# Retention and cosine MLP on one core: the first k in two transfers, part of the first v on another queue, and a new plan

## The chip, the cores and the metric

The kernel runs on one core of a Trainium2 chip. The metric is the time of one execution on the device, in microseconds (us), lower is better. The kernel before took 209.12 us, the median of three runs (208.57 to 209.28). A profiled execution took 208.1 us, of which the profile's span covers 206.3. All times of single instructions below are from that profile.

## The reference

Two layers follow each other. The first is a recurrent retention over 768 time steps, for 4 batch elements and 8 heads of 64 channels; the second multiplies its output (3072 tokens of 512) by w_in (512 x 2048), applies h * cos(h), and multiplies by w_out (2048 x 512).

```python
for t in range(S):
    state = gamma * state + k[t] (outer) v[t]
    y[t] = scale * q[t] @ state
x = y as (tokens, heads * channels)
h = x @ w_in
out = (h * cos(h)) @ w_out
```

All inputs and the output are float32.

## The kernel before

**Tiles.** Time is cut into 6 chunks of 128 steps, and the batch into 2 pairs. A slot p is one chunk of one pair, so there are 12 slots; slots 0 and 1 are the first chunk of each pair. In a slot, the recurrence becomes matrix products: q and k are transposed on TensorE (`t_mm`, line 361) and copied back (`t_copy`), the scores of each head are multiplied (`a_mm`, line 399 for the first two slots, 389 later), masked with the decay (`a_mask`, or `a_save` and `a_late` through ScalarE and GpSimd), and multiplied with v (`y_first`, line 431, for the first two slots; `y_block` later). The state between chunks is kept in one PSUM bank (`s_mm`, line 578). The output of a slot is copied, transposed, into `xt` (`y_copy`).

**The MLP.** Two slots make a group of 512 tokens. A unit of work multiplies 512 tokens by 128 columns of w_in (`f_mm`, line 590), or, where only one slot is there yet, 256 tokens by two times 128 columns (`h_mm`, line 611). ScalarE takes the cosine (`f_cos`), VectorE the product (`f_mul`, `h_mul`), and `o_mm` (line 635) multiplies by w_out. `HALF0` says how many of the 16 column blocks of group 0 are done as half units.

**Loads.** q of slot 0 comes by SyncE's hardware queue in two halves, one for each batch element of the pair. Nearly everything else in the first 60 us is issued by GpSimd, through the software queue: `load(p, "K")` or `"Q"` casts to bf16 on the way (slots 0 and 1), `"q"`, `"k"`, `"v"` bring float32, which an engine converts (`conv_q`, `conv_k`, `conv_v`, and `raw_v`, a plain cast of v for slots 0 and 1). Names with a digit, such as `q0`, load one batch element; in the kernel before, only q is loaded so. GpSimd works through its instructions in order, so issues, conversions and masks stand in one line there.

**The plan.** The order of the first half (slots 0 to 6, group 0 and the start of group 1) is made while the kernel is built: `Plan.run` is a list scheduler with a cost for each operation, tokens for PSUM banks and buffers, a rank for each operation, and assumed times of landing (`ld`, `at`). The constants `SHIFT` and `ON` change ranks and choose engines; they were searched for. Where TensorE has nothing to do between 4.2 and 18 us of the plan's own time, it puts in `idle_mm` (line 664), a product of zeros into a free bank that keeps the array running. The instructions are then emitted in the plan's order, and the chip keeps only this order, not its times: every engine executes in order and waits on semaphores. From group 2 on the order is a fixed loop.

**What the change touches:** the loads of slot 0 (`load`, and the two calls ahead of the plan), the table of assumed landings `ld` and the list `LOADS`, the constants, and with them the order of the whole planned half.

Of the kernel before, what the change touches and what calls it, by code (L numbers as in the profile page):

```python
# [161 lines left out]
            op["fn"](op["eng"])  # L162


HOLD = ""
SHIFT = {"ml010": 25.5, "mulf0.2": -74.7, "f0.3": 0.3, "cosf0.2": -11.6, "cosf0.3": -2.2, "mulf0.3": -4.9, "f0.2": 2.8, "m011": -20.0, "mulh1.4": -20.5, "m000": 82.7, "cosf0.5": -41.6, "ck21": 45.1, "a31": -124.5, "m100": 2.2, "f0.5": 23.0, "a5": -2.5, "v0": -97.2, "ms110": 6.4, "ml110": -41.8, "cosf0.4": -0.9, "f0.4": -9.8, "mulf0.5": 16.9, "eq51": 13.1, "m110": 64.4, "t20": -21.1, "k5": -46.0, "mulf0.8": 31.6, "yc21": -50.4, "f0.6": 2.1, "f0.7": 55.3, "ek10": -92.1, "w0b": -22.2, "a21": -34.2, "h1.0": 81.4, "cosh2.2": 3.0, "m501": 38.5, "yc30": -23.3, "ml011": -27.8, "mulf0.15": 5.8, "sc5": 79.1, "m201": -81.3, "mulh2.2": -18.0, "oc1": -45.8, "mulf0.14": -66.8, "cq31": -32.2, "mulf0.9": -47.9, "mulf0.6": 5.7, "cosf0.7": -27.8, "a30": -8.1, "cosf0.6": -7.2, "h0.2": -12.1, "eq21": -4.6, "cq51": 3.2, "cq41": 38.6, "f0.14": 23.8, "ek20": -13.4, "yc50": 39.8, "cv51": 23.4, "ek51": 88.5, "mulh2.10": 23.3, "cq70": 8.6, "f0.10": -46.0, "mulf0.13": 1.5, "h1.6": 5.9, "ml100": 20.1, "f0.15": 60.8, "o2.1": -8.1, "h3.10": 31.9, "t51": 14.8, "h3.0": -7.1, "h3.14": 28.8, "cq00": -2.7, "m601": 4.7, "h1.4": 1.8, "eq11": 37.0, "cosf0.12": -60.7, "v6": -26.4, "m400": 17.7, "mulh3.12": 67.0, "w2": 49.4, "sw": -53.6, "cv10": -0.0, "rv00": 14.5, "mulh2.8": 4.5, "ek50": 72.2, "cosf0.11": 2.4, "m101": -34.4, "h2.2": 1.1, "q2": -22.9, "q5": -59.7, "cosh3.14": 19.9, "y3": 19.8, "t40": 30.7, "o2": -0.8, "mulh3.4": -0.3, "cq40": -13.2, "mulh0.2": -29.3, "y5": -35.7, "mulh3.14": -25.5, "h2.12": -50.9, "oc0": -94.2, "a10": 39.9, "ek11": -35.3, "h0.6": 6.9, "eq40": -6.2, "h2.6": 58.1, "rv10": -9.1, "dt71": -1.3, "cosh3.8": -31.0, "cosh0.2": 18.8, "cv70": -67.6, "o3.1": -13.8, "cq60": -11.1, "ck60": 71.1, "m511": 10.9, "sc4": -15.9, "o1.3": -16.8, "m510": 4.5, "k4": 12.5, "h0.4": -9.2, "cq71": 3.6, "mulh3.2": 58.9, "cosh1.2": -26.7, "mulh3.6": -1.4, "cv61": 13.7, "o2.2": -9.8, "q6": -7.4, "o0.2": -7.5, "mulh2.4": 44.5, "mulh2.6": 22.6, "mulh3.10": 16.6, "v5": -53.7, "cq61": 27.8, "o1.1": -27.2, "ck61": 0.2, "m200": -10.8, "cosf0.9": 6.3, "cosh0.4": 11.6, "q4": 78.9, "cosh3.6": -6.8, "h1.2": -87.9, "tq01": 1.8, "oc3": -74.8, "mulh0.0": -16.9, "eq01": 11.2, "t21": 6.2, "ck41": 29.7, "cosh3.4": 9.3, "oc2": 8.6, "m211": 23.9, "cq01": -56.9, "w0a": 17.8, "o1.0": -7.7, "yc01": 2.2, "k7": 54.8, "yc51": -0.7, "cosf0.13": -14.9, "cosh2.10": -36.4, "yc00": 7.1, "cosh1.4": -13.4, "ek00": -8.7, "m611": -13.9, "tk10": -101.4, "mulh0.4": -40.7, "mulf0.10": 15.2, "m600": -35.2, "a00": -17.4, "cosh2.0": -5.5, "m301": 18.6, "rv11": -50.0, "sc0": -52.0, "ek01": -31.6, "cv01": 13.3, "ek21": -3.2, "cosf0.10": 7.2, "v7": -2.1, "ek40": 18.1, "t31": 22.7, "mulh1.6": 0.2, "eq30": -9.4, "y4": 19.2, "tk11": 1.9, "ek31": -26.9, "w3b": 23.5, "cosh2.12": -0.2, "cosh0.6": 4.7, "cosh2.8": -4.4, "cosh3.2": 25.8, "cv60": 2.7, "cosh2.4": -14.4, "v4": -1.1, "mulh2.12": 36.6, "dt61": -8.8, "eq41": -12.5, "mulf0.11": 31.8, "ek41": -0.8, "eq50": 9.1, "a11": -23.9, "yc10": 9.3, "o0.3": 0.3, "dt60": -3.3, "o3.3": 50.5, "mulh2.14": -42.3, "m610": -12.1, "f0.11": -0.6, "s0": 3.1, "cv11": 38.9, "h3.8": -17.4, "yc40": 14.3, "m410": -8.4, "h2.8": -4.0, "m300": 15.8, "o0": -14.6, "cv31": -27.4, "rv01": 0.6, "cosf0.14": 2.4, "cosh2.6": 11.7, "cv50": -6.8, "m010": -1.2, "ms011": -12.0, "f0.13": -5.2, "l8": 5.1, "ck70": 3.2, "t41": 1.0, "o1.2": -2.3, "cv71": 0.5, "tq11": 31.2, "h2.4": -3.6, "mulh0.6": 8.8, "t50": 7.1, "ck31": 42.7, "yc20": -52.3, "m001": -4.7, "y01": 62.0, "y2": 15.3, "f0.12": 20.5, "ms111": 2.0, "mulh1.2": -13.9, "cosh3.10": -49.0, "ck51": -9.0, "h0.0": -0.1, "eq31": 1.4, "eq20": -5.1, "q7": 1.5, "cosh3.0": 6.2, "cosh3.12": 1.5, "cv40": 2.3, "y11": 3.6, "o1": -24.4, "cv00": -1.4, "sc2": -3.2, "m411": 18.0, "m210": -8.1, "v3": 0.0, "eq10": 1.1, "tk01": 22.8, "yc41": -25.6, "cq21": -1.8, "f0.9": -31.4}
ON = {"cv70": "P", "cv00": "D", "cv30": "D", "cv31": "D", "cv60": "D", "cv11": "D", "cv10": "P", "rv01": "D", "sc5": "D", "rv11": "A", "yc20": "D", "sc3": "D", "eq40": "DA", "eq50": "A", "rv00": "A", "yc00": "D", "yc31": "DA", "ek51": "D", "ek11": "DA", "sc4": "D", "ek20": "A", "cv61": "P", "eq01": "DA", "cv51": "D", "ek41": "D", "eq41": "A", "cv20": "P", "yc01": "DA", "eq20": "A", "eq30": "DA", "ek50": "D", "ek00": "D", "sc2": "DA", "yc50": "DA", "yc40": "A", "yc21": "A", "cq21": "D", "ek40": "DA", "cv01": "D", "cv71": "P", "cv21": "P", "ek21": "DA", "cv41": "P", "cq20": "D", "ek10": "DA", "yc30": "A", "ek01": "D"}
HALF0, SPARE, RF, RM, COLD = 8, 1, 50.0, 50.0, 5.2


@with_exitstack
def kernel(
# [9 lines left out]
    nc = tc.nc  # L182
    B, H, S, D = q.shape
# [9 lines left out]
    PRE = 5  # L193
# [70 lines left out]
    def kb(p):  # L264
        return by_b(kx if p == 1 else ks[p % NB], p)
# [6 lines left out]
    def load(eng, p, names):  # L272

        bp, c = divmod(ORDER[p], NC)
        for n in names.split():
            t, src = SRC[n[0].lower()]
            if len(n) == 1:
                t = (qb(p) if n == "Q" else kb(p)) if n in "QK" else t[p % PRE]  # L280
                eng.dma_start(  # L281
                    out=t.rearrange("p b h d -> p (b h) d"),
                    in_=src[ds(2 * bp, 2), :, ds(c * C, C), :].rearrange(
                        "b h t d -> t (b h) d"))
            elif n[1] == "s":
                fl = t[p % PRE].rearrange("p b h d -> p (b h) d")
                for x in range(2):
                    for lo, n4, th in ((0, 4, x), (4, 8, 1 - x), (12, 4, x)):
                        eng.dma_start(
                            out=fl[ts(x, 64), ds(lo, n4), :],  # L290
                            in_=src[ds(2 * bp, 2), :, ds(c * C + 64 * th, 64), :]
                            .rearrange("b h t d -> t (b h) d")[:, ds(lo, n4), :])
            else:
                b = int(n[1])
                eng.dma_start(
                    out=t[p % PRE][:, b],
                    in_=src[2 * bp + b, :, ds(c * C, C)].rearrange("h t d -> t h d"))

    def load_w_in(lo, n):
# [362 lines left out]
    def idle_mm(e, n=1):  # L662
# [10 lines left out]
                   allow_small_or_imprecise_dtypes=True)  # L673
    nc.gpsimd.iota(far[:, 8:24], pattern=[[1, 16]], base=0, channel_multiplier=0,
                   allow_small_or_imprecise_dtypes=True)
    load(nc.sync, 0, "q0 q1")
    load(nc.gpsimd, 0, "K")
    nc.vector.memset(zero, 0.0)
    nc.vector.memset(lnsc, math.log(scale))
    nc.vector.memset(halfpi, math.pi / 2.0)  # L680
# [2 lines left out]
        out=dist.rearrange("p (a b) -> p a b", a=8),  # L683
# [20 lines left out]
    PL = 6  # L704
    ASEP = 4
    MERGE = 4
    CQ, CD = "P", "DP"
    SPLIT = {(1, 1, 1), (0, 1, 1)}
    HM, HCQ, HCV = "q2", "", ""
    plan = Plan({"bank": 7, "cos": 3, "sem": 8, "out": 4, "port": 1, "ring": 7}, 6.5)  # L710
    add = plan.add
    SB2 = {"D": (0.33, 0.42), "A": (0.49, 0.585)}
    TT = {"D": (0.6, 0.69), "P": (1.03, 1.05)}
# [1 line left out]
    ld = {}  # L715
    prev = None
    at = lambda tm: dict(start=0.0, free=0.0, done=tm, lat=0.0)
    ld["q", 0, 0], ld["q", 0, 1], ld["k", 0, 0], ld["k", 0, 1] = map(at, (3.9, 5.0, 7.4, 7.4))
    LOADS = ["Q1", "K1", "v0", "v1", "w0a", "w0b", "w1", "w2", "q2", "k2", "w3a", "v2", "w3b", "o0", "q3", "k3", "v3", "o1", "q4", "o2", "k4", "v4", "q5", "k5", "o3", "v5", "q6", "k6", "v6", "q7", "k7", "v7"]
    LAG = {"w1": 0.15}  # L720
    pend = []
    for i, x in enumerate(LOADS):
        if x[0] in "qkvQK":
            p = int(x[1:])
            o = add("P", 1.2, lambda e, p=p, n=x[0]: load(nc.gpsimd, p, n),
                    [("issued", prev)] if prev else [], 50 + i if p < 7 else 45,
                    [("sem", 1), ("ring", 1)], [("sem", 1), ("ring", 1)], mb=524288e-6, rate=330e-3, name=x)
            ld[x[0].lower(), p, 0] = ld[x[0].lower(), p, 1] = o
            if p >= PRE:
                pend.append((o, x[0], p - PRE))  # L730
        elif x[0] == "w":
# [16 lines left out]
    for p in range(PL + 2):  # L748
# [92 lines left out]
        else:  # L841
# [4 lines left out]
                    name="y%d" % p)  # L846
# [151 lines left out]
```

## Time and profile before

| engine | busy us | share of the span |
|---|---|---|
| TensorE, matmuls (PE) | 201.4 | 98% |
| TensorE, weight loads (PEld) | 108.6 | 53% |
| VectorE (DVE) | 114.2 | 55% |
| ScalarE (ACT) | 115.2 | 56% |
| GpSimd (POOL) | 73.8 | 36% |

| landing at the start | issued by | first used at us |
|---|---|---|
| q of slot 0, first batch element | SyncE | 3.76 |
| q of slot 0, second | SyncE | 4.64 |
| k of slot 0 | GpSimd, from 1.41 for 1.38 us | 7.17 |
| q of slot 1 | GpSimd, 2.79 | 8.86 |
| k of slot 1 | GpSimd, 3.92 | 10.71 |
| v of slot 0 | GpSimd, from 5.06 | 12.23 |
| v of slot 1 | GpSimd, after it | 13.94 |

How to read it: an engine that is busy for 98% of the span sets the time, but busy is not the same as useful. The 34 products of zeros are in the 201.4 us as well: seven while the kernel starts, the others between 4.26 and 15.19 us. The second table gives the time of the first instruction that reads the data, which may be later than the landing. In tables of stretches of time ("windows") the columns are: the stretch, its length, the busy time of PE, PEld, DVE, ACT and POOL with the number of instructions, the granted clock of TensorE, the mean share of busy DMA engines (over 1 where transfers overlap), and GB/s written. A line of waits has the engine and line that waited, what ended the wait, the sum in us, the count and the longest.

### The profile page before, as it was taken

What the parts mean: (1) busy time and instruction counts of PE and PEld (TensorE: products, weight loads), DVE (VectorE), ACT (ScalarE), POOL (GpSimd) and SP (SyncE); (2) the same over time, 40 slices, a digit from 0 to 9 for tenths busy, and PEclk for the clock granted to TensorE, in tenths of its full rate; (3) what the DMA queues carried; (4) which work ended last, traced back from release to release, by engine and by line L of the source; (5) the groups of instructions that cost most, each with busy time, mean ns of one, the idle gap of its engine ahead of it and who ended that gap; (6) DMA issues with size and microseconds to landing.
All of it is one profiled execution on the core that took longest, in us unless ns stands there. A gap on an engine that the chain in (4) does not pass through costs nothing.

```text
span 206.3 us, 5229 instructions
## 1 busy us (share of the span) xinstructions
PE 201.4 (98%) x2178; PEld 108.6 (53%) x2178; DVE 114.2 (55%) x194; ACT 115.2 (56%) x193; POOL 73.8 (36%) x77
## 2 busy tenths in 40 slices
PE   7999999999999999999999999999999999999994
PEld 2558656868945545445445445454444444444442
DVE  5589897866996548338338438448442444444000
ACT  7567886859855357547546546554555553554120
POOL 8969979899973004305207005200000000000000
PEclk9999999999999999999999999999999999999999
DMA  7999999999998976876877675501101101110212
GB/s 121 186 262 210 314 241 312 255 342 276 344 312 150 231 158 175 201 193 171 192 177 144 151 193 142 153 0 56 53 1 51 51 3 51 51 51 0 104 53 102
DMA packets 58600, 32.15 MB, mean 156 GB/s; under 512 B 47696, under 2 KB 53072, under 8 KB 58576
## 3 DMA queue, kind: packets, MB, share of 16 engines
q0 software_dynamic: 14352, 15.47, 33.9%
q1 hardware_dynamic: 44080, 16.28, 31.1%
q8 instruction: 17, 0.28, 0.6%
q10 hardware_dynamic: 144, 0.07, 0.1%
q14 instruction: 7, 0.06, 0.1%
HBM read 27.26 MB, written 6.29 MB: 163 GB/s over the span
## 4 chain that ended last, share of the span: by engine, by line
PE 78%; DMA 10%; POOL 7%; DVE 2%; issue 1%; ACT 1%; POOLq 0%; DVEq 0%
PE bank L635 37%; PE bank L590 27%; DMA vf<-in_v_dram 10%; PE bank L611 4%; PE bank L389 2%; PE bank L480 2%; PE bank L655 2%; DVE gt L619 1%; PE st_ps L508 1%; POOL qf L281 1%; POOL kf L281 1%; PE bank L494 1%; PE bank L361 1%; POOL w_in_sb L300 1%; POOL ks L281 1%
## 5 line engine op out<-in xcount | busy, mean ns | idle before, releaser
L598 ACT ACTIVATE cosb<-bank,halfpi 128x512 bf16<-128x512 f32 x96 | 65.6, 690 | 53.2 <-PE bank L590 48.0
L635 PE MATMUL bank<-w_out_sb,gt 128*128 128x512 bf16 x368 | 90.9, 379 | 0.0
L602 DVE TENSOR_TENSOR gt<-bank,cosb 128x512 bf16<-128x512 f32 x72 | 49.1, 690 | 55.8 <-ACT cosb L598 55.7
L590 PE MATMUL bank<-xt,w_in_sb 128*128 128x512 bf16 x288 | 73.2, 379 | 0.0
L635 PEld LDWEIGHTS <-gt 128*128 128x128 bf16 x368 | 35.5, 98 | 42.3 <-issue 0.2
L590 PEld LDWEIGHTS <-w_in_sb 128*128 128x128 bf16 x288 | 27.6, 98 | 32.3
L324 POOL TENSOR_TENSOR qs<-qf,gq 128x512 bf16<-128x512 f32 x18 | 18.5, 1044 | 43.5 <-PE bank L480 22.6
L408 DVE TENSOR_TENSOR am<-bank,mask 128x512 bf16<-128x512 f32 x40 | 24.8, 682 | 4.2 <-PE bank L389 4.2
L313 ACT COPY ob<-bank 128x512 f32<-128x512 f32 (+1 forms) x24 | 14.0, 582 | 16.0 <-PE bank L635 13.9
L611 PE MATMUL bank<-xt,w_in_sb 128*128 128x256 bf16 x192 | 22.3, 273 | 0.0
L611 PEld LDWEIGHTS <-w_in_sb 128*128 128x128 bf16 x192 | 18.5, 98 | 3.1
L619 DVE TENSOR_TENSOR gt<-bank,cosb 128x512 bf16<-128x512 f32 x24 | 16.0, 686 | 4.7 <-ACT cosb L598 4.6
L313 ACT CAST xt<-bank 128x512 bf16<-128x512 f32 x21 | 11.4, 588 | 10.8 <-PE bank L480 10.1
L313 ACT CAST ks<-kf 128x512 bf16<-128x512 f32 x20 | 11.5, 625 | 2.7 <-DMA kf<-in_k_dram 2.7
L664 PE MATMUL bank<-zero 128*128 128x512 bf16 x34 | 10.5, 442 | 1.1 <-DVE halfpi L680 1.1
L480 PE MATMUL bank<-am,vs 64*64 64x128 bf16 (+1 forms) x320 | 10.3, 206 | 0.1
L336 POOL TENSOR_TENSOR vs<-vf,gk 128x512 bf16<-128x512 f32 x8 | 8.9, 1113 | 3.3 <-PE bank L480 1.5
L331 POOL TENSOR_TENSOR vs<-vf,gk 128x512 bf16<-128x512 f32 x8 | 8.2, 1042 | 5.2 <-DMA vf<-in_v_dram 3.8
L281 POOL DMA_DIRECT2D vf<-in_v_dram x8 | 9.4, 1182 | 1.0 <-DVE vs L336 0.8
L315 DVE CAST stb<-st_ps 128x512 bf16<-128x512 f32 x9 | 6.2, 687 | 3.8 <-PE st_ps L508 3.3
L389 PE MATMUL bank<-qkt 64*64 64x128 bf16 (+1 forms) x320 | 8.0, 206 | 0.3 <-ACT qkt L313 0.2
L313 ACT COPY qkt<-bank 128x512 bf16<-128x512 bf16 x13 | 7.1, 592 | 1.8 <-PE bank L361 1.2
(66 smaller groups left out, 132.7 us busy)
## 6 DMA issues: line engine op xcount, KB each, us to landing
out_dram<-ob SPq DMA_DIRECT2D x23, 256.0 KB, 2.4
vf<-in_v_dram POOLq DMA_DIRECT2D x8, 512.0 KB, 12.0
qf<-in_q_dram POOLq DMA_DIRECT2D x6, 512.0 KB, 12.5
kf<-in_k_dram POOLq DMA_DIRECT2D x6, 512.0 KB, 12.4
w_out_sb<-in_moe_w_out_dram POOLq DMA_DIRECT2D x4, 512.0 KB, 14.1
qf<-in_q_dram SPq DMA_DIRECT2D x4, 512.0 KB, 4.6
w_in_sb<-in_moe_w_in_dram POOLq DMA_DIRECT2D x4, 256.0 KB, 8.7
w_in_sb<-in_moe_w_in_dram POOLq DMA_DIRECT2D x2, 512.0 KB, 10.5
```

The source lines that it names most:

```text
L281: eng.dma_start(out=t.rearrange("p b h d -> p (b h) d"), in_=src[ds(2 * bp, 2), :, ds(c * C, C), :].rearrange("b h t d -> t (b h) d"))
L313: nc.scalar.copy(out=out, in_=in_)
L324: ENG[e].tensor_tensor(out=qb(p)[:, b], in0=qf[p % PRE][:, b], in1=bc(gq, ORDER[p] % NC), op=ALU.mult)
L389: return nc.tensor.matmul(ap[b][ts(x, 64), a, lo:], lhsT=kt(p % NB, b, h)[:, ts(x, 64)], rhs=qt(p % NB, b, h)[:, lo:], tile_position=(64 * ...
L408: nc.vector.tensor_tensor(out=am[p % 2][b][u], in0=bank.rearrange("p (a t) -> p a t", a=HP), in1=(dec[:, b] if p < 2 else mask[second(p, 0 ...
L480: m = nc.tensor.matmul(held["yp", p][b][ts(j, 64), a, lo:], lhsT=vs[p % NB][ts(r, 64), b, h, :], rhs=am[p % 2][b][h // 4][ts(r, 64), h % 4 ...
L590: nc.tensor.matmul(bank, lhsT=w_in_sb[:, i, ts(f, 128)], rhs=xt[g % 2][:, i, :], start=(i == 0), stop=(i == KIN - 1))
L598: nc.scalar.activation(out=cb, in_=bank, func=AF.Sin, bias=halfpi)
L602: nc.vector.tensor_tensor(out=gt[g % 2][:, f, :], in0=bank, in1=cb, op=ALU.mult)
L611: nc.tensor.matmul(bank[:, ts(e, 256)], lhsT=w_in_sb[:, i, ts(f + e, 128)], rhs=xt[g % 2][:, i, ts(hf, 256)], start=(i == 0 and e == 0), s ...
L619: nc.vector.tensor_tensor(out=gt[g % 2][:, f : f + 2, ts(hf, 256)], in0=bank.rearrange("p (f t) -> p f t", f=2), in1=cb.rearrange("p (f t) ...
L635: nc.tensor.matmul(bank, lhsT=gt[g % 2][:, f, ts(j, 128)], rhs=w_out_sb[:, f, :], start=(f == 0), stop=(f == KOUT - 1))
```

## The change

k of slot 0 is loaded by two software transfers, one for each batch element, so that the first half can be issued, and used, before the second. v of slot 0 is split as well: its first batch element goes to SyncE's hardware queue, behind q; its second stays with GpSimd, in the place of the whole. The assumed landings follow: k at 6.4 and 6.9 (7.4 for both before), v's first element at 9.0, the software stream from 5.9 on (6.5 before). The list of loads gets another order: the first half of w_in's first 512 columns comes ahead of v of slot 1, and later weights move forward. `HALF0` falls from 8 to 4. With these, the plan's ranks and engines were searched for anew (`SHIFT`, `ON`, left out here).

```diff
-HOLD = ""
...
-HALF0, SPARE, RF, RM, COLD = 8, 1, 50.0, 50.0, 5.2
+HOLD = "P"
...
+HALF0, SPARE, RF, RM, COLD = 4, 0, 40.0, 50.0, 5.2
...
-                    out=t[p % PRE][:, b],
+                    out=(kb(p) if n[0] == "K" else t[p % PRE])[:, b],
...
-    load(nc.sync, 0, "q0 q1")
-    load(nc.gpsimd, 0, "K")
+    load(nc.sync, 0, "q0 q1 v0")
+    load(nc.gpsimd, 0, "K0 K1")
...
-    CQ, CD = "P", "DP"
-    SPLIT = {(1, 1, 1), (0, 1, 1)}
+    CQ, CD = "P", "P"
+    SPLIT = {(1, 1, 0), (0, 1, 1)}
...
-    plan = Plan({"bank": 7, "cos": 3, "sem": 8, "out": 4, "port": 1, "ring": 7}, 6.5)
+    plan = Plan({"bank": 7, "cos": 3, "sem": 8, "out": 4, "port": 1, "ring": 7}, 5.9)
...
-    ld["q", 0, 0], ld["q", 0, 1], ld["k", 0, 0], ld["k", 0, 1] = map(at, (3.9, 5.0, 7.4, 7.4))
-    LOADS = ["Q1", "K1", "v0", "v1", "w0a", "w0b", "w1", "w2", "q2", "k2", "w3a", "v2", "w3b", "o0", "q3", "k3", "v3", "o1", "q4", "o2", "k4", "v4", "q5", "k5", "o3", "v5", "q6", "k6", "v6", "q7", "k7", "v7"]
+    ld["q", 0, 0], ld["q", 0, 1], ld["k", 0, 0], ld["k", 0, 1] = map(at, (3.9, 5.0, 6.4, 6.9))
+    ld["v", 0, 0] = at(9.0)
+    LOADS = ["Q1", "K1", "v0", "w0a", "v1", "w0b", "w1", "w2", "q2", "w3a", "k2", "w3b", "v2", "o0", "o1", "q3", "k3", "v3", "o2", "q4", "o3", "k4", "v4", "q5", "k5", "v5", "q6", "k6", "v6", "q7", "k7", "v7"]
...
-            o = add("P", 1.2, lambda e, p=p, n=x[0]: load(nc.gpsimd, p, n),
+            half = x == "v0"
+            o = add("P", 0.7 if half else 1.2,
+                    lambda e, p=p, n="v1" if half else x[0]: load(nc.gpsimd, p, n),
...
-            ld[x[0].lower(), p, 0] = ld[x[0].lower(), p, 1] = o
+            for b in range(half, 2):
+                ld[x[0].lower(), p, b] = o
```

In the new list, `"v0"` stands for the second batch element of v of slot 0 alone.

## The prediction

> **What bounds the kernel now.** I read the page's first two parts first, then the windows of the start, then the timeline of TensorE, and last the waits of TensorE.
>
> ```profile
> PE 201.4 (98%) x2178; PEld 108.6 (53%) x2178; DVE 114.2 (55%) x194; ACT 115.2 (56%) x193; POOL 73.8 (36%) x77
> ...
> DMA  7999999999998976876877675501101101110212
> ```
>
> TensorE is busy for 201.4 of 206.3 us. The rest is 1.06 us ahead of its first instruction, 2.6 us of final write-out after its last, and about 1 us of gaps. So it is the bound, and the only ways to be faster are fewer useless matmuls and fewer gaps. Useless ones exist: line 664 multiplies zeros into a free bank, to keep the array running while nothing is there to compute.
>
> ```profile
> 13.00 0.64 PE L431 MATMUL bank<-am,gt 128*64 128x128 bf16 x16
> 13.57 1.69 PE L664 MATMUL bank<-zero 128*128 128x512 bf16 x7
> 15.19 0.64 PE L431 MATMUL bank<-am,gt 128*64 128x128 bf16 x16
> 15.76 1.92 PE L611 MATMUL bank<-xt,w_in_sb 128*128 128x256 bf16 x16
> 17.61 0.44 PE L578 MATMUL st_ps<-vs,ks 128*64 128x64 bf16 x16
> ```
>
> This is TensorE's timeline (start, length). L431 is the output of slot 0, then of slot 1; L611 is the first real w_in work. From 15.19 on there is no filler. Between 4.26 and 15.19 there are 27 fillers (groups of 2, 7, 2, 4, 3, 2 and 7). So the start is limited by landings, and the rest by TensorE's own work.
>
> ```profile
> 2.50:4.00 1.50, 1.50 (x5) 0.30 (x2) 0.68 (x9) 1.50 (x6) 1.50 (x3) 1.00 1.27 283
> 4.00:5.00 1.00, 0.97 (x6) 0.56 (x6) 0.56 (x2) 1.00 (x5) 1.00 (x1) 1.00 1.34 109
> 5.00:9.00 4.00, 3.96 (x42) 1.98 (x41) 1.82 (x5) 2.26 (x6) 4.00 (x6) 1.00 2.39 153
> 9.00:10.00 1.00, 1.00 (x12) 0.62 (x10) 1.00 (x3) 0.96 (x2) 1.00 (x2) 1.00 1.97 252
> 10.00:12.50 2.50, 2.14 (x30) 1.15 (x29) 1.52 (x4) 0.86 (x2) 1.64 (x2) 1.00 1.07 341
> ```
>
> The last column is GB/s written. k of slot 0, q and k of slot 1 are cast to bf16 on the way, so 153 written is 306 read: from 5 us on the DMA engines run at one rate, about 300 GB/s of source data. From 4 to 5 us, where k of slot 0 is the only long transfer, they do 109 (at most 218 read). That hole, and the wait of k for its descriptors, is what the change can win.
>
> ```profile
> PE bank L664 <- DVE halfpi L680: 1.1, 1, 1.1
> PE bank L361 <- DMA kx<-in_k_dram: 0.4, 1, 0.4
> PE bank L389 <- ACT qkt L313: 0.2, 1, 0.2
> ```
>
> TensorE's waits: after the start only 0.6 us in all. The present order is kept almost exactly by the chip.
>
> **What the Trainium skill says.** "DMA: Bandwidth & Descriptors", section "Specifications", gives about 1 us to the first byte on the software path and 0.6 us on the hardware path. The trace agrees in kind: k's issue ends at 2.79 us, and the written rate shows bf16 only from about 4.0. The same page, "Queues, rings and completion order", says that each DMA engine takes turns between the queues that it has work for, packet by packet. The trace is mixed: the small copies of gk and mask, issued by SyncE from 5.21 us, took 6.0 to 6.4 us to land, all that time beside the software stream. "TensorE: Matmul & The Clock Gate", section "What's actually happening", gives 215.7 ns from start to start of warm matmuls of 512 columns; four of L590 take 0.86 us in the chain here, 216 ns each, so a filler costs 0.216.
>
> **The change part by part.**
> *k of slot 0 in two software transfers.* The whole issue took 1.38 us on GpSimd, later ones of this kind 1.17; no row shows a half: between 0.59 (half of 1.17) and 0.8 (a w_in issue), I take 0.7. The first half is then issued by some 2.2 us instead of 2.79, and its data starts 0.6 earlier, inside the hole. k landed at 7.17 (first matmul on it); the first half should now land 0.8 to 1.1 us earlier, the second 0 to 0.5. GpSimd pays two halves for one whole, nothing.
> *v of batch element 0 on SyncE, behind q.* A third issue of 0.54 us (1.08 for two) behind which only the gk and mask copies wait, needed much later: free. It takes 256 KB out of the software stream. When does it land? At best one q half after q's second, 4.64 + 0.88 = 5.5; at worst it is held back like the gk copies, till the casts end at about 9.5, so at about 10.4. It is first read by a cast on ScalarE, wanted for slot 0's output, which in the new order comes right after the transposes of k of slot 1 (10.7 before). Both ends are early enough, so I charge nothing on that path. But the bytes are moved all the same: if v takes its turns early, 256 KB at 300 GB/s, 0.87 us, is put ahead of k, q1 and k1, against 0.6 us won from the earlier start. So the casts land between 0.6 earlier (v held back) and 0.3 later (v served at once).
> *Order of loads: the first half of w_in's first 512 columns now ahead of v of slot 1.* In the old order v1 was the sixth load and landed by 13.94 (its cast starts there with no wait). Now 512 KB of w_in stand ahead of it, 1.3 us (from 15 to 20 us, where only w_in is loaded, the window of the trace has 206 GB/s of bf16 written, 412 read). 13.94 + 1.3 - 0.6 = 14.6 if v's other half is moved ahead of it as before; 0.87 less, 13.8, if that half finds only idle turns. Two casts on ScalarE (1.14) then precede slot 1's output: 14.95 to 15.75.
> *HALF0 8 to 4.* 32 fewer of L611 (0.109 each, from the 40 between 17.98 and 22.36) and 16 more of L590 (0.216): -3.49 + 3.46, nothing.
> *Fillers.* Compared instruction by instruction, TensorE's other counts are the same in both. The fillers fall from 34 to 27, all in the start: 2, 3, 2, 2, 4, 1, 5 and 1 instead of the 27 above. And one group of 8 L611 stands ahead of slot 1's output. 7 x 0.216 = 1.51 us less work. TensorE would reach slot 1's output at 15.19 - 1.51 + 0.87 = 14.55, instead of 15.19, with 0.87 us of w_in work already done.
> *What of it remains.* At 14.55 TensorE asks for v1's cast, which is there at 14.95 to 15.75, while the second half of that output would be due at 14.87 (half of its 0.64 later): 0.1 to 0.9 us lost. I take 0.45, near the middle. The next wait could be GpSimd: in its new order a masked product, two issues (1.2 and 0.8) and v's scaling (1.05) precede slot 0's state update, which is ready near 17.3 if k1 lands at 10.8, while TensorE comes there at about 17.0 to 17.4. The late cases of the two are the same landing, so they don't add.
> *GpSimd.* Two more q conversions than before, 2 x 1.04 us, less about 0.5 for a half issue. From 30 to 60 us it is busy 27.9 of 30. It then waits 13.15 us for TensorE, so I charge nothing; the high end, 1.6, goes to the range.
> *The other reordering* (some 300 shifted ranks): no counts change, TensorE's order was without gaps from 16 us on and is assumed to stay so.
> Sum: 209.12 - 1.51 + 0.45 = 208.06, so 208.1.
>
> **Rivals.**
> (a) The landings come as the table in the code has them (k 6.4 and 6.9, v 9.0), and the waits of 0.4 and 0.2 go too: 209.12 - 1.51 - 0.3 = 207.3. For it: the old table's k (7.4) agrees with the trace (7.17) within 0.25 us. Against it: no bytes are saved, and the new table has the stream both 0.6 earlier and relieved of v.
> (b) No change: v1 and the state update are late by the whole 0.9, and a further 0.5 is lost where the weights, now read earlier because HALF0 is 4, arrive just in time (w_in columns 512 and up read at about 18.3, landing there before at about 19). 209.0.
> (c) Slower. v on the hardware queue is starved as the gk copies were and lands after 12 us; ScalarE, in order, holds the copies of slot 1's transposes behind it, and TensorE stands 2 us; or GpSimd's added work is in the path of slots 2 to 5 (DMA at 9 tenths and GpSimd at 93% until 60 us leave little to catch up with). 209.12 - 1.51 + 2.5 to 3 = 210.1 to 210.6. For it: 6.0 to 6.4 us for tiny copies. Against it: they were queued when the software queue was already deep, and v is queued before it starts.
>
> **How the numbers follow.** Forecast 0.45, (a) 0.24, (b) 0.15, (c) 0.16. 0.3% is 0.63 us: faster means below 208.5. Of the forecast about 0.8 lies there, the whole of (a), little of (b): 0.62. Same: 0.21. Slower: 0.17. The range, 207.0 to 209.8, takes in (a), (b) and the high end of GpSimd's cost, and leaves out most of (c).
>
> **What would show it.** In the profile after: 27 matmuls of L664; k of slot 0 read by TensorE before 6.7 us; v of the first batch element landing between 5.5 and 10.4 us with no wait of ScalarE on it; the first L611 near 13.5 and the last filler before 14.6; a wait of L431 on ScalarE's cast of 0.1 to 0.9 us, the largest of TensorE's waits. Right in size if TensorE is without gaps from 17.5 us on. It is wrong if TensorE waits in sum over 1 us between 16 and 70 us, on GpSimd's conversions, on w_in, or on q, k or v loads, or if the cast of v's first half holds up ScalarE.

## The result, and the profile after

The changed kernel took 210.73 us (median; the kernel before 209.16 beside it), a ratio of 1.0079 with a 95% interval of 1.0059 to 1.0099: slower by 1.6 us, where 1.0 us faster was forecast. A repetition gave 1.0124 (1.0092 to 1.0156). Executions more than 1.5% above the fastest of their kernel are left out of every ratio here; as the first profile (216.58 us) fell in one, the profile shown is that of a later execution of 210.94 us (span 209.2, clock 1.000), with a second one (209.79 us, span 208.0) beside it.

The page's first two parts, as shown of before:

```profile
PE 199.4 (95%) x2132; PEld 106.2 (51%) x2155; DVE 117.3 (56%) x194; ACT 114.2 (55%) x191; POOL 76.5 (37%) x80
...
DMA  8999999999976785776775986701101101110212
```

TensorE has less to do and a longer span: its share fell from 98% to 95%. (The 23 matmuls fewer than weight loads are missing records.) Its longest waits (the sum in us, the count and the longest):

```profile
PE bank L611 <- DVE gt L619: 1.1, 1, 1.1
PE bank L664 <- DVE halfpi L680: 1.1, 1, 1.1
PE bank L361 <- DVE qs L315: 0.9, 2, 0.6
PE bank L361 <- DMA kx<-in_k_dram: 0.8, 1, 0.8
PE bank L361 <- DMA ks<-in_k_dram: 0.7, 1, 0.7
```

Three waits of the start (on q's cast, on k of slot 1, on k of slot 0) sum to 2.4 us, against 0.4 before; and one of 1.1 us (L611) stands in the middle, on a product of VectorE. The start, in TensorE's timeline:

```profile
6.87 0.39 PE L361 MATMUL bank<-ident,ks 128*128 128x128 bf16 x4
7.10 0.59 PE L664 MATMUL bank<-zero 128*128 128x512 bf16 x2
8.36 0.40 PE L361 MATMUL bank<-ident,ks 128*128 128x128 bf16 x4 [0.66 <-DMA ks<-in_k_dram]
...
12.33 0.62 PE L361 MATMUL bank<-ident,kx 128*128 128x128 bf16 x8 [0.83 <-DMA kx<-in_k_dram]
...
14.45 1.25 PE L664 MATMUL bank<-zero 128*128 128x512 bf16 x5
15.54 1.04 PE L611 MATMUL bank<-xt,w_in_sb 128*128 128x256 bf16 x8
16.41 0.38 PE L664 MATMUL bank<-zero 128*128 128x512 bf16 x1
16.72 0.69 PE L431 MATMUL bank<-am,gt 128*64 128x128 bf16 x16
```

k's first half is used at 6.87 (7.27 in the second profile), its second only at 8.36 (8.46). Slot 1's output begins at 16.72; the kernel before had it at 15.19, and at 15.54 in a second profile of it. 0.87 us of w_in work stand ahead of it now, so with that work counted as done TensorE is late by 0.3 to 0.7 us there; the forecast, counted alike, had it 1.51 us early.

The windows, first the start and the stretch from 50 to 60 us of the changed kernel, then that stretch of the kernel before:

```profile
5.00:9.00 4.00, 3.02 (x31) 1.42 (x29) 2.02 (x4) 1.90 (x5) 4.00 (x5) 1.00 2.09 173
9.00:10.00 1.00, 0.95 (x14) 0.34 (x10) 0.80 (x2) 0.38 (x1) 0.24 (x1) 1.00 2.35 154
...
50.00:60.00 10.00, 8.68 (x106) 7.09 (x105) 10.00 (x14) 7.01 (x13) 9.14 (x9) 1.00 1.03 346
```

```profile
50.00:60.00 10.00, 10.00 (x115) 7.64 (x113) 8.21 (x15) 8.31 (x15) 9.08 (x9) 1.00 1.04 341
```

From 50 to 60 us VectorE (the third busy time) has no free moment, 10.00 of 10 for 14 instructions, and TensorE (the first) loses 1.3 us (0.64 in the second profile); before, VectorE was busy 8.21 for 15 instructions and TensorE without a gap.

For the comparison of many profiles I cut the span at three of TensorE's weight loads: the first of slot 1's output, the first of the fixed loop, and the first of the last output (`last_o`, L655). In us:

| kernel | to slot 1's output | to the loop | to the last output | to the end |
|---|---|---|---|---|
| before | 15.19 | 55.63 | 128.62 | 6.88 |
| before, second profile | 15.54 | 55.58 | 128.54 | 6.89 |
| changed (210.94 us) | 16.72 (15.85 without the w_in work done early) | 56.47 (57.34 with it) | 128.70 | 7.28 |
| changed (209.79 us) | 16.70 (15.83) | 55.47 (56.34) | 128.57 | 7.28 |

So there are three losses: 0.3 to 0.7 us in the start, 0.7 to 1.8 in the planned middle, and 0.39 after the last output's first matmul. The two executions of the kernel before in this table (208.1 and 208.33 us) lie 0.5 to 1.1 us under its medians (208.8 to 209.2), so the table makes the first two losses look larger than the ratios do.

### The profile page after: what moved, and what is told of

Same layout as the page of the kernel before. It is cut to its first block, busy times and chain, and to the rows that moved or that the text cites. A ratio compares the mean times of both kernels' runs of the same rounds, so it can differ in the third digit from the quotient of the medians.

```text
span 214.8 us, 5179 instructions
## 1 busy us (share of the span) xinstructions
PE 203.2 (95%) x2155; PEld 107.6 (50%) x2155; DVE 121.4 (57%) x194; ACT 114.4 (53%) x191; POOL 76.4 (36%) x80
## 4 chain that ended last, share of the span: by engine, by line
PE 86%; DVE 7%; DMA 4%; POOL 2%; issue 1%; POOLq 0%; DVEq 0%
PE bank L635 37%; PE bank L590 31%; PE bank L611 5%; DVE vs L336 4%; DMA kx<-in_k_dram 4%; PE bank L389 2%; PE bank L480 2%; PE bank L361 2%; PE bank L655 2%; PE st_ps L508 2%; DVE gt L619 1%; PE bank L494 1%; POOL ks L295 1%; DVE am L408 1%; PE bank L664 1%
## 5 line engine op out<-in xcount | busy, mean ns | idle before, releaser
L635 PE MATMUL bank<-w_out_sb,gt 128*128 128x512 bf16 x368 | 92.3, 384 | 0.0
L590 PE MATMUL bank<-xt,w_in_sb 128*128 128x512 bf16 x304 | 76.5, 380 | 0.0
L590 PEld LDWEIGHTS <-w_in_sb 128*128 128x128 bf16 x304 | 29.1, 98 | 34.4
L324 POOL TENSOR_TENSOR qs<-qf,gq 128x512 bf16<-128x512 f32 x20 | 21.4, 1085 | 41.3 <-PE bank L480 31.3
L313 ACT COPY ob<-bank 128x512 f32<-128x512 f32 (+1 forms) x24 | 13.9, 581 | 16.5 <-PE bank L635 14.4
L611 PE MATMUL bank<-xt,w_in_sb 128*128 128x256 bf16 x160 | 18.8, 273 | 1.1 <-DVE gt L619 1.1
L611 PEld LDWEIGHTS <-w_in_sb 128*128 128x128 bf16 x160 | 15.3, 98 | 3.8 <-issue 1.3
L619 DVE TENSOR_TENSOR gt<-bank,cosb 128x512 bf16<-128x512 f32 x20 | 13.4, 681 | 3.2 <-ACT cosb L598 3.1
L336 DVE TENSOR_TENSOR vs<-vf,gk 128x512 bf16<-128x512 f32 x7 | 12.2, 1747 | 0.0
L313 ACT CAST ks<-kf 128x512 bf16<-128x512 f32 x20 | 11.7, 621 | 0.2 <-DMA kf<-in_k_dram 0.2
L331 POOL TENSOR_TENSOR vs<-vf,gk 128x512 bf16<-128x512 f32 x8 | 8.2, 1042 | 8.6 <-DMA vf<-in_v_dram 8.6
L664 PE MATMUL bank<-zero 128*128 128x512 bf16 x27 | 9.6, 476 | 1.1 <-DVE halfpi L680 1.1
L336 POOL TENSOR_TENSOR vs<-vf,gk 128x512 bf16<-128x512 f32 x7 | 7.3, 1049 | 7.5 <-PE bank L480 7.1
L361 PE MATMUL bank<-ident,qs 128*128 128x128 bf16 x48 | 5.2, 242 | 4.5 <-DVE gt L619 3.8
```

The lines of the kernel that those rows point to most:

```text
L313: nc.scalar.copy(out=out, in_=in_)
L324: ENG[e].tensor_tensor(out=qb(p)[:, b], in0=qf[p % PRE][:, b], in1=bc(gq, ORDER[p] % NC), op=ALU.mult)
L336: ENG[e].tensor_tensor(out=vb(p)[:, b], in0=vf[p % PRE][:, b], in1=bc(gk, ORDER[p] % NC), op=ALU.mult)
L590: nc.tensor.matmul(bank, lhsT=w_in_sb[:, i, ts(f, 128)], rhs=xt[g % 2][:, i, :], start=(i == 0), stop=(i == KIN - 1))
L611: nc.tensor.matmul(bank[:, ts(e, 256)], lhsT=w_in_sb[:, i, ts(f + e, 128)], rhs=xt[g % 2][:, i, ts(hf, 256)], start=(i == 0 and e == 0), s ...
L619: nc.vector.tensor_tensor(out=gt[g % 2][:, f : f + 2, ts(hf, 256)], in0=bank.rearrange("p (f t) -> p f t", f=2), in1=cb.rearrange("p (f t) ...
```

## The experiments

**Theories.** A ("theory P" in the expectations): what the plan keeps apart does not stay apart on the chip. VectorE's conversions of v (`conv_v`, L336) and GpSimd's conversions of q (`conv_q`, L324) run into each other at 50 to 60 us. The planner keeps them apart by a token, `[("port", 1)], [("port", 1)], name="cv%d%d" % (p, b))`, but only in its own time; the chip keeps the order on each engine alone. In the kernel before, GpSimd did both v conversions of slot 4 itself, so that these could not meet its conversions of q:

```profile
46.62 1.05 POOL L336 TENSOR_TENSOR vs<-vf,gk 128x512 bf16<-128x512 f32 x1
...
48.82 1.05 POOL L336 TENSOR_TENSOR vs<-vf,gk 128x512 bf16<-128x512 f32 x1
```

The new plan gives them to VectorE. B ("theory L"): the new transfers bring the data later, and all the rest follows from that. C: the other order of loads (w_in ahead of v of slot 1).

**Again the changed kernel.**

> The changed kernel once more, for its profile. Both theories: 210.6 us. Theory L (landings at the start): k of slot 1 and v of slot 1 first used about 2 us later than before, and nearly all of the 1.6 us is lost before 20 us. Theory P (the later plan): TensorE also stands for 0.5 us or more between 45 and 66 us, with VectorE's v conversions (0.68 us alone) stretched over GpSimd's.

1.0124 (1.0092 to 1.0156). Its VectorE has stretched conversions too (1.20 and 1.85 us, where one alone takes 0.68), and 0.5 us of TensorE's waits is on a product behind them.

**The transfers apart from the plan.** Old transfers in the new order:

```diff
-    load(nc.sync, 0, "q0 q1 v0")
-    load(nc.gpsimd, 0, "K0 K1")
+    load(nc.sync, 0, "q0 q1")
+    load(nc.gpsimd, 0, "K")
...
-                    lambda e, p=p, n="v1" if half else x[0]: load(nc.gpsimd, p, n),
+                    lambda e, p=p, n="v" if half else x[0]: load(nc.gpsimd, p, n),
```

> The new order, but k of slot 0 in one software transfer and v of slot 0 whole by software, as before. Theory L: the landings of k and of slot 1 come back to 7.2 and 10.7, and the time falls by 1 to 2 us, to 208.6 to 209.6. Theory P: the order's own collisions stay, and the time stays at 210.2 to 211.

210.67 us, 1.0091 (1.006 to 1.0122): the two ratios of the changed kernel, 1.0079 and 1.0124, lie on both sides of it, so the transfers alone don't explain the loss. It rests on four executions; the two at a clock of 1.000 took 210.1 and 210.3 us. k landed at 7.2 and k of slot 1 at 10.6, as before the change; but v of slot 0, whole and by software, came at 12.3, and its cast is the largest wait of TensorE now:

```profile
PE bank L431 <- ACT gt L313: 1.6, 1, 1.6
```

Slot 1's output begins at 16.79. VectorE's four conversions in the middle took 1.42, 1.57, 1.23 and 0.92 us. The reverse is the new transfers in the old order:

```diff
-                    out=t[p % PRE][:, b],
+                    out=(kb(p) if n[0] == "K" else t[p % PRE])[:, b],
...
-    load(nc.sync, 0, "q0 q1")
-    load(nc.gpsimd, 0, "K")
+    load(nc.sync, 0, "q0 q1 v0")
+    load(nc.gpsimd, 0, "K0 K1")
...
-            o = add("P", 1.2, lambda e, p=p, n=x[0]: load(nc.gpsimd, p, n),
+            o = add("P", 1.2, lambda e, p=p, n="v1" if x == "v0" else x[0]: load(nc.gpsimd, p, n),
```

> The order of before, but with k of slot 0 in two transfers and half of v of slot 0 on SyncE's queue. Theory L: the start is 1 to 2 us late as in the changed kernel, and the old order has 7 more fillers, so 210.5 to 211.5. Theory P: the old order takes the late start without collisions later, 209.2 to 210.2.

209.99 us, 1.0065 (1.0042 to 1.0089). Here the transfers cost 1.1 to 1.4 us: slot 1's output begins at 17.01, with the old order's fillers all in place, and 7.28 us pass from the last output to the end. No conversion of v is stretched between 50 and 63 us (0.68 each). B is thus true of the start, and not of the changed kernel's middle.

**Which half of the transfers.** Only k split, v of slot 0 whole by software:

```diff
-    load(nc.sync, 0, "q0 q1 v0")
+    load(nc.sync, 0, "q0 q1")
...
-                    lambda e, p=p, n="v1" if half else x[0]: load(nc.gpsimd, p, n),
+                    lambda e, p=p, n="v" if half else x[0]: load(nc.gpsimd, p, n),
```

> The new order with k in two transfers, but v of slot 0 whole by software. Theory L in the form 'v on the hardware queue takes turns from the casts': k's second half used at 7.2 to 7.5 instead of 8.9, k of slot 1 at 11, time 208.6 to 209.6. In the form 'the second issue of k costs as much as the whole': k's second half and all behind it still 0.6 us late, 209.6 to 210.4. Theory P: 210.2 to 211.

Only v split, k whole:

```diff
-    load(nc.gpsimd, 0, "K0 K1")
+    load(nc.gpsimd, 0, "K")
```

> The new order with half of v of slot 0 on SyncE's queue, but k of slot 0 in one software transfer. If the second issue of k (0.9 us) is what makes slot 1 late: q and k of slot 1 land at 9.2 and 11.3 us instead of 10.1 and 12.3. If it is v's turns on the hardware queue: they stay within 0.3 of 10.1 and 12.3. The time, 209.8 to 211, does not tell the two apart.

1.0119 (1.0075 to 1.0163) and 1.0118 (1.0071 to 1.0166), each from two executions only, so the two can't be told from each other or from the changed kernel. Their landings can be read (us; of the changed kernel two profiles; TensorE's clock in the profile with only k split was 1.00 up to 13 us and 0.70 from 13 to 16):

| landing | before | changed | k split only | v split only |
|---|---|---|---|---|
| k of slot 0, first, second half | 7.1 | 6.8, 8.4 | 6.1, 6.9 | 8.5 |
| q of slot 1 | 8.8 | 10.0, 10.1 | 9.7 | 10.2 |
| k of slot 1 | 10.6 | 12.3 | 11.5 | 12.3 |
| v of slot 0, first element (SyncE) | 12.3 | 7.8 | 13.0 | 7.3 |
| v of slot 1 | 13.8 | 15.8, 15.9 | 16.1 | 16.0 |

The halves of k land early when v isn't on the other queue (6.1 and 6.9, where the whole had 7.1), and k is late when v is (8.5 whole). Each part alone puts off q and k of slot 1, the split of k by 0.9 us and v by 1.4 to 1.7; they don't add. What was expected of v's turns on the hardware queue (10.1 and 12.3 with k whole) came true. "DMA: Bandwidth & Descriptors", section "Queues, rings and completion order", of the Trainium skill says that a DMA engine takes turns between its queues packet by packet; that agrees with the changed kernel, where v lands at 7.8, between the two halves of k (6.8 and 8.4), at the cost of k. The landings vary by themselves: two kernels with the same transfers up to there, the old transfers in the new order above and the exchange of two loads below, had k landed at 7.2 and at 8.0 and k of slot 1 at 10.6 and at 11.7, so 1 us in one row of one profile is not yet a finding.

**The order of two loads.** This kernel has the old transfers in the new order, and in addition w_in's first half and v of slot 1 change places:

```diff
+    named = {o["name"]: o for o in plan.ops}
+    x, y = named["w0a"], named["v1"]
+    x["fn"], y["fn"] = y["fn"], x["fn"]
```

> As e_oldloads (new order, old transfers of slot 0), but v of slot 1 is issued ahead of the first half of w_in again. If the place of v of slot 1 is what delays the start: it lands at 13.8 instead of 15.3, TensorE's wait of 1.6 us for its cast shrinks under 0.6, and the useless time up to 20 us is 0.5 to 0.9 less; 209.8 to 210.2 in all. If not: the start stays as it is, 210.4 to 211.

211.78 us, 1.0108 (1.0073 to 1.0144): not faster, a miss, so nothing supports C. TensorE's wait of 1.6 us stayed, because it was for v of slot 0 (13.4 here), in front of which nothing had moved; as k itself landed at 8.0, the whole start was late in this profile.

**The collision taken away, first way.** The changed kernel with three conversions of q (slot 5, and the first element of slot 6) replaced by a write of zeros on GpSimd; q of slot 5 and half of q of slot 6 are zero in it.

```diff
+    for o in plan.ops:
+        if o["name"] in ("cq50", "cq51", "cq60"):
+            o["fn"] = lambda e, n=o["name"]: nc.gpsimd.memset(qb(int(n[2]))[:, int(n[3])], 0.0)
```

> The changed kernel, but GpSimd clears q of slot 5 and half of slot 6 instead of converting it, so those outputs are not the reference's. These three conversions run beside VectorE's v conversions at 52 and 57 us. If the collision[...] is the later loss: VectorE's stretched 1.2 and 1.85 us fall to under 0.8, and TensorE loses 0.5 to 0.9 us less between 50 and 62 us. If it is VectorE's amount of work: at most 0.2 less.

209.33 us, 1.0007 (0.9993 to 1.002). First VectorE's, then GpSimd's timeline of the changed kernel (start, length), then both of this one:

```profile
50.86 1.55 DVE L336 TENSOR_TENSOR vs<-vf,gk 128x512 bf16<-128x512 f32 x1
52.33 0.41 DVE L315 COPY qkt<-bank 128x512 bf16<-128x512 bf16 x1
52.66 1.92 DVE L336 TENSOR_TENSOR vs<-vf,gk 128x512 bf16<-128x512 f32 x1
54.51 0.68 DVE L619 TENSOR_TENSOR gt<-bank,cosb 128x512 bf16<-128x512 f32 x1
```

```profile
50.72 1.19 POOL L281 DMA_DIRECT2D vf<-in_v_dram  x1 [0.45 <-DMA qf<-in_q_dram]
51.93 1.37 POOL L324 TENSOR_TENSOR qs<-qf,gq 128x512 bf16<-128x512 f32 x1
...
56.76 2.51 POOL L324 TENSOR_TENSOR qs<-qf,gq 128x512 bf16<-128x512 f32 x2
```

```profile
51.06 0.68 DVE L336 TENSOR_TENSOR vs<-vf,gk 128x512 bf16<-128x512 f32 x1
51.66 0.42 DVE L315 COPY qkt<-bank 128x512 bf16<-128x512 bf16 x1
51.99 0.68 DVE L336 TENSOR_TENSOR vs<-vf,gk 128x512 bf16<-128x512 f32 x1
```

```profile
50.90 1.19 POOL L281 DMA_DIRECT2D vf<-in_v_dram  x1 [0.45 <-POOL vx L336]
52.09 0.54 POOL L925 MEMSET qs<- 128x512 bf16 x1
```

The two conversions took 1.55 and 1.92 us in the changed kernel and 0.68 each here, where GpSimd's writing of zeros lies right over the second. GpSimd's issue of a transfer (L281) lies over the first in both kernels, so it alone is not the cause. The product behind them (L619 at 54.51) is what TensorE waits for in the changed kernel, 1.06 us ahead of its L611 at 55.24; here that wait is gone.

**Second way, all work kept.** Both v conversions of slot 4 go to GpSimd as well:

```diff
+    for o in plan.ops:
+        if o["name"] in ("cv40", "cv41"):
+            o["eng"] = "P"
```

> The changed kernel with both v conversions of slot 4 on GpSimd instead of VectorE, in the same places of the order. Collision theory: no stretched VectorE instruction at 52 us, 0.3 to 0.6 us faster than the changed kernel. If GpSimd is the bound of that stretch: its two more conversions of 1.04 us make it slower by 0.5 to 2 us.

209.41 us, 1.0015 (0.9997 to 1.0032), though GpSimd has more to do (9.96 of 10 us from 50 to 60). As both conversions are GpSimd's own work now, the two engines hardly get in each other's way (of VectorE's two remaining ones, one took 0.68 and one 0.93). GpSimd's timeline has them at their undisturbed length:

```profile
50.67 1.05 POOL L336 TENSOR_TENSOR vs<-vf,gk 128x512 bf16<-128x512 f32 x1
...
52.87 1.06 POOL L336 TENSOR_TENSOR vs<-vf,gk 128x512 bf16<-128x512 f32 x1
```

From slot 1's output to the loop it took 55.09 us, 1.4 less than the first profile of the changed kernel and 0.4 less than the second; with the zeros it took 54.91. The same edit with the old transfers, and a run of the kernel before for scale:

> The new order with both v conversions of slot 4 on GpSimd, and the transfers of slot 0 as before. If, with the collisions gone, the new transfers still cost: 0.3 to 0.9 us faster than with them (209.4). If the new transfers do what the new order needs (an early v for ScalarE): the same or slower, 209.4 to 210.2.

> The kernel before once more, for a second profile: the first one took 208.1 us, 1 us under its median. Equal in time, ratio 1.000. If the landings at the start vary from run to run, its first uses of k and of slot 1 are later than 7.2 and 10.7 us; if not, they agree within 0.2.

209.15 us, 1.0033 (1.0013 to 1.0052), against 210.67 with the collision; and for the kernel before again 0.9995 (0.9972 to 1.0019). With both sets of transfers the edit gives 1.2 to 1.3 us back by the ratios (1.0079 to 1.0015 and 1.0091 to 1.0033); from the repetition's 1.0124 it would be 2.3. Without the collision the two sets of transfers can't be told apart. The two ways close the two rivals: in the first VectorE has as much to do as before, and in the second GpSimd has more, so neither engine's amount of work is the cause.

**The reverse in the kernel before.** Does it suffer if VectorE gets these two conversions?

```diff
+    for o in plan.ops:
+        if o["name"] in ("cv40", "cv41"):
+            o["eng"] = "D"
```

> The kernel before, but with both v conversions of slot 4 on VectorE, in the same places, as the changed kernel has them. Collision theory: stretched conversions of over 1 us on VectorE between 45 and 58 us, and 0.5 to 1.5 us slower than before. If the changed kernel's loss needs its late start as well: within 0.3 us of before.

208.89 us, 1.0007 (0.9985 to 1.0028): no, and the stretched conversions that were expected did not come. The conversions lie at 46.93 and 49.75 there, 0.68 us each, while GpSimd issues transfers or stands still, and the one at 59.25 took 0.88. So VectorE can have this work at no cost as long as it does not meet GpSimd's; as nothing meets here, the run does not test the collision itself.

**An earlier first load.** With the second way, `load(nc.gpsimd, 0, "K0 K1")` moved ahead of the small index patterns of GpSimd, to win the start too:

> The changed kernel with both v conversions of slot 4 on GpSimd, and with the two issues of k ahead of GpSimd's three index patterns. k should land 0.4 to 0.5 us earlier, and if the transfers that follow are limited by bytes, v of slot 1 too: 209.0. If they are limited by GpSimd's issues, which follow at the same times as before, only k is early: 209.4.

209.94 us, 1.0049 (1.0022 to 1.0076), a miss. What is made from those patterns (`ident`, which the transposes need, among it) is late, VectorE's first cast of q behind it also, and TensorE stands:

```profile
PE bank L361 <- DVE qs L315: 2.1, 1, 2.1
```

**More profiles.**

> The changed kernel, a third look: its profile so far is of its fastest run (209.8 us, median 211). If the collisions vary from run to run, the fixed loop starts later than 72.2 us by as much as VectorE's v conversions are stretched more; k of slot 1 is used at 12.3, v of slot 1 at 15.9, both within 0.4.

> New order, k in two transfers, v whole by software, a second look. If v on the hardware queue is what delays the casts: k's second half is used at 7.5 or earlier and k of slot 1 at 11.6 again, 0.7 or more ahead of the changed kernel on the same chip.

> New order, k in one transfer, half of v on SyncE's queue, a second look. If the second issue is what delays the casts: k of slot 1 is used at 11.3 or earlier; if v's turns on the hardware queue: at 12.3, as in the changed kernel.

> New order with the transfers of before, a second look: k of slot 0 used at 7.2 to 8.0, k of slot 1 at 10.7 to 11.3, v of slot 1 at 15.3, the fixed loop from 73.0 us on, with VectorE's v conversions between 50 and 60 us stretched to over 1 us.

The first is the profile shown above. Beside the execution of 209.79 us it has the same start (16.72 and 16.70 us) and 1.0 us more up to the loop, and its four conversions of the middle took 5.27 us in sum against 4.41. So of these two the longer one has the worse collision. The second profile (k split only) has k landed at 6.0 and 6.9 and k of slot 1 at 11.4, about as before, and v of slot 0 late again. The third (v split only) has k at 8.7 and k of slot 1 at 12.5.

The last two took 216.76 and 216.1 us, and they and the profile of 216.58 us show the collision at its worst. In all three, VectorE's fourth conversion takes 4.93 us: it begins ahead of four instructions of GpSimd that follow each other without a gap, and ends only after the last of them. VectorE, then GpSimd, in the profile of 216.58 us:

```profile
59.12 4.93 DVE L336 TENSOR_TENSOR vs<-vf,gk 128x512 bf16<-128x512 f32 x1
```

```profile
59.46 1.03 POOL L336 TENSOR_TENSOR vs<-vf,gk 128x512 bf16<-128x512 f32 x1
60.46 2.03 POOL L324 TENSOR_TENSOR qs<-qf,gq 128x512 bf16<-128x512 f32 x2
62.46 1.03 POOL L336 TENSOR_TENSOR vs<-vf,gk 128x512 bf16<-128x512 f32 x1
```

TensorE waits 3.8 to 4.2 us for the product behind it. Of the 31 executions of the kernels that keep the collision, nine took over 216 us; of the 82 of the kernels without it, none took over 211. So the 1.3 us found above are not all that the collision can cost.

**The last 0.4 us.** All six kernels so far with v's half on SyncE's queue have 7.27 to 7.29 us from the last output to the end, all others 6.88 to 6.92. The lines of the change are 190 us away from there. The trace shows what differs: at the end SyncE waits for the semaphores one after the other, in an order fixed when the kernel is built, 0.06 us each. In the kernel before, ScalarE's last store of 64 KB signals the last of them; in the changed kernel it signals the third, with seven waits left behind it (the expectation below counted six). In the traces, successive hardware transfers signal successive semaphores, so one transfer more moves all later ones by one place. The first test gives the kernel before one further hardware transfer, by cutting one store of the fixed loop in two:

```diff
-        nc.sync.dma_start(out=out[ds(o_row(g, j), C), :], in_=held.pop(("dma", g, j)))
+        o = held.pop(("dma", g, j))
+        for lo, n in (((0, 256), (256, 256)) if (g, j) == (3, 0) else ((0, 512),)):
+            nc.sync.dma_start(out=out[ds(o_row(g, j), C), ds(lo, n)], in_=o[:, ds(lo, n)])
```

> The kernel before, with the output store of one tile (group 3, first 128 tokens) cut into two SyncE transfers of 256 columns, in the fixed loop where SyncE has time. In all kernels so far that load half of v of slot 0 by SyncE, 7.27 to 7.28 us pass from the first of the last output's matmuls (L655) to the end of the span; in all without it 6.88 to 6.91. Theory: at the end SyncE waits for one semaphore of each kind in a fixed order, about 0.06 us each, and a further transfer on a hardware queue shifts which of them the last store (ScalarE's 64 KB) gets: last in the list before (nothing left behind it), third in the list after (six waits left behind it, 0.38 us). Then one further hardware transfer anywhere does the same: 7.27 us here, and about 0.4 us on the whole, 209.2 to 209.5. Rival: the 0.39 us belongs to v's transfer itself or to the data's place; then 6.89 us here and no change of the time.

The second test takes the kernel of the second way above and gives it one hardware transfer fewer, as one such store is issued by GpSimd:

```diff
-        nc.sync.dma_start(out=out[ds(o_row(g, j), C), :], in_=held.pop(("dma", g, j)))
+        e = nc.gpsimd if (g, j) == (3, 0) else nc.sync
+        e.dma_start(out=out[ds(o_row(g, j), C), :], in_=held.pop(("dma", g, j)))
```

> The changed kernel with both v conversions of slot 4 on GpSimd, and the output store of one tile (group 3, first 128 tokens) issued by GpSimd's software queue in place of SyncE's, so that the number of hardware transfers is that of the kernel before. Theory (order of the final waits): 6.89 us from the first L655 to the end instead of 7.27, and 0.38 us less than the 209.41 of the same kernel without this edit, 209.0. Rival (v's transfer itself): 7.27 us and 209.4.

The first: 7.27 us to the end, 209.67 in all, 1.0031 (1.0015 to 1.0046). The second: 6.88 us, 208.88 in all, 1.0002 (0.9987 to 1.0018). So the rival (v's own transfer) falls. The waits of SyncE at the end show it, in this order for the kernel before, the changed one, the one with a transfer more, and the one with a transfer fewer:

```profile
SPq L993 <- DMA out_dram<-ob: 1.5, 2, 1.0
```

```profile
SPq L998 <- DMA out_dram<-ob: 1.9, 1, 1.9
```

```profile
SPq L995 <- DMA out_dram<-ob: 1.9, 1, 1.9
```

```profile
SPq L1002 <- DMA out_dram<-ob: 1.5, 2, 1.0
```

Two waits mean that SyncE comes through its list to the last stores and waits for one after the other; one wait of 1.9 us means that it is held early in the list, for the store that lands last, with the rest still to do. No version was faster than the kernel before; the last one equals it.

## Why the prediction was wrong, step by step

Three terms failed. TensorE's order after the start was "assumed to stay" without gaps and GpSimd's new work was charged nothing, and there the collision costs about 1.3 us. The start was charged 0.45 us for late data, and it lost 2.15. A further hardware transfer was called free, and it costs 0.39 us at the end.

- *k in two transfers.* I took 0.7 us for the issue of a half; the two took 1.09 and 0.89, 1.98 in sum for 1.38 of the whole. Everything behind is issued 0.6 us later (q of slot 1 at 3.38 for 2.79). "GpSimd pays two halves for one whole, nothing" failed. The first half was used at 6.9 to 7.3, at best 0.3 earlier, not 0.8 to 1.1; the second 1.2 us later, not earlier. That is v's doing: with only k split the halves landed 1.0 and 0.2 us ahead of the whole, as forecast for k alone.
- *v's half on SyncE.* It landed at 7.8, within 5.5 to 10.4, and ScalarE never waited for it: right. But q and k of slot 1 came 1.2 to 1.7 us later, where I had "0.6 earlier to 0.3 later". Two terms were off. The issue's term has the wrong sign, 0.6 later instead of 0.6 earlier. And v's own term, 0.87 us of bytes, was too small: v alone, with k's issue as before, put q and k of slot 1 off by 1.4 and 1.7 us. Their sum, 1.5, comes near the measured delay, but the runs with one part each don't add in this way, so that is partly luck.
- *The order of loads.* v of slot 1 came at 15.8 to 15.9, forecast 13.8 to 14.6. The delay of 1.5 us just named accounts for it; that w_in goes first was costed about rightly (13.9 + 1.3 - 0.9 + 1.5 = 15.8).
- *HALF0.* Charged nothing. No run changed it alone, and no gap in the traces points to it.
- *Fillers.* There are 27, which is 1.51 us less work. But fillers stand where TensorE would wait anyway, and they are not what sets the arrival: TensorE came to slot 1's output at 16.7, 2.15 us after the 14.55 forecast, having waited 2.4 us for k and q. The term "+0.45" for what remains should have been 2.15 (1.7 more). No wait of L431 was seen, since TensorE's order put fillers and w_in work where it would have stood.
- *GpSimd's conversions and the other reordering.* "I charge nothing", "TensorE's order was without gaps from 16 us on and is assumed to stay so": this failed as well, by about 1.3 us, as the two ways of taking the collision away show. I had looked at GpSimd's busy time and at counts, but not at which engine has which conversion, and which of GpSimd's instructions and VectorE's fall at one time. That the high end of 1.6 was of the right size was luck: the reason is not that GpSimd had more to do (with still more it is faster), but that VectorE's conversions were now beside its own.
- *The end.* The "third issue" on SyncE was called free. It costs 0.39 us at the end of the program, which the profile before alone, without one of another count of transfers beside it, could hardly have told.
- *The sum.* -1.51 + 2.15 (start) + 1.3 (collision) + 0.39 (end) is +2.3; the measured ratios are +1.6 and +2.6 us. The start's part, 0.64 of it, is the least sure: the last version (the second way, with one transfer fewer) comes as late to slot 1's output (16.81) and yet equals the kernel before within 0.4 us. Rival (a) took 0.3 off for two waits that sum to 0.6. Rival (c) named a slower result with GpSimd's work in the path of slots 2 to 5, and 210.1 to 210.6, near the outcome; v, its first reason, was not starved.

The Trainium skill, "SBUF — State Buffer", section "Who interferes with whom", states that a product of VectorE with both inputs in SBUF contends with a GpSimd instruction that reads SBUF, and not with one that only writes. The traces agree on both sides: 0.68 us became 0.88 to 1.92 with L324 beside it, and stayed 0.68 beside the writing of zeros. It was there to be used in the prediction, and I didn't.

What stays open: how much of the stretch each GpSimd instruction makes (its spans in the profile are rough, and by them the conversion at 50.86 us should have been over before L324 begins at 51.93); why the delays by k's split and by v don't add in the landings; and how much of the late start is left at the end.

## What to carry over

When a change is a new order, compare not only counts and busy times, but which instructions of engines that share something fall at the same time, and ask how late each may come before they meet. A plan that keeps two engines apart in its own time does so only as long as the landings keep to it. Cutting a transfer in two is not free where its issue has a fixed part. A further transfer anywhere can move the end of the program, so compare the last microseconds as well. And read the longest executions too: here they held the clearest picture of the cause.

## What the runs showed of the hardware that I had not expected

- A software transfer's issue on GpSimd has a large fixed part: it took 1.38 us for k whole, 1.09 and 0.89 for its halves, 1.20 for v whole and 0.93 for half of it. From the two figures of v, my estimate is 0.66 fixed and 0.27 for each half.
- VectorE's two q casts of the start took 0.84 to 1.17 us each, where they took 0.44 to 0.70 before. GpSimd issues transfers beside them in both kernels, but the split of k makes the difference: with k split at least one of the two took 0.97 to 1.19 us in each of nine profiles, while with k whole, v on SyncE's queue or not, none took over 0.77 in ten. (In the kernel with k ahead of the index patterns the casts come 2 us later, and none took over 0.79.)
- In the kernel before, a conversion at 15.57 us took 1.53 us while GpSimd only issued transfers, but at 51.06 us, in the kernel with zeros, one lay within an issue and took 0.68. So issues stretch some and not others; the runs don't show which.
- The order of the final waits on semaphores is worth 0.39 us: seven waits of 0.06 us stand behind the last store or ahead of it.
- A VectorE product can be held through a whole run of GpSimd instructions: 4.93 us instead of 0.68, in three profiles.
